# One level of Strassen in the second product of a fused attention and feed-forward kernel

## Chip, cores, metric

The kernel runs on one core of one Trainium2 chip. The metric is the device time of one execution in microseconds. The kernel before takes 303.68 us (median of 3 runs, 303.0 to 303.9). The span in a profile is 1.7 to 2.2 us shorter than the time of the same run.

## The reference

```python
# attention in chunks of 64 tokens: q, k, v are (8, 8, 576, 64), float32
scores = (1 / sqrt(64)) * q_c @ k_c.T;  attn = softmax(scores);  out = attn @ v_c
x = out.transpose(0, 2, 1, 3).reshape(4608, 512)
h = x @ w_in                       # 512 -> 2048
g = np.maximum(0.01 * h, h)
return g @ w_out                   # 2048 -> 512, float32
```

## The kernel before

The 4608 tokens go through in nine blocks of 512. TensorE runs the first product of block j (16 groups of 4 matmuls, `mm1`), then its second product (4 token groups of 16 matmuls, `mm2`). Between these groups, at fixed steps n, stand the four attention stages of block j+1 for each of four head pairs: `attn_t` (copies of q and k into matmul form, on VectorE), `attn_s` (scores), `attn_x` (sums and attn @ v) and `attn_n` (normalise into `xT`, on VectorE). GpSimd casts k, half of v and, up to block 3, q of later blocks to fp16; from block 4 on VectorE casts q. From block 3 on, the DMA transposes q and k; before that TensorE does.

```python
KD = [...]                                 # two block-diagonal buffers of k
def attn_t(j, kk):
    ...                                    # j < 3: TensorE transposes into PSUM (tp), VectorE copies qt
    for hh in range(2):                    # two copies of kd, 64 x 512 each
        nc.vector.tensor_copy(out=dst, in_=src)      # block 0: partly on ScalarE

def mm1_end(j, hp, fc):                    # ScalarE: leaky ReLU into g, fp16
    nc.scalar.activation(out=gT[j][:, fc, :], in_=hp, func=AFT.Prelu, ..., alpha=0.01)

def mm2(j, ti, part):                      # 4 matmuls of 512 columns
    for fc in range(part * 4, part * 4 + 4):
        nc.tensor.matmul(out=o, lhsT=gT[j][:, fc, ti * 128:(ti + 1) * 128],
                         rhs=w_out[:, fc, :], start=(fc == 0), stop=(fc == NFC - 1))
    if part == 3:
        nc.vector.tensor_copy(out=osb, in_=o)        # PSUM -> SBUF, then stored by DMA

for j in range(NJ):
    qk_at = {0: {26: 2}, 1: {0: 3, 29: 4}, 2: {15: 5}}.get(j, {9: j + 3})   # step: block whose q, k are loaded
    ...
    for n in range(...):                   # program order of all engines
        mm1(j, n) or mm2(j, ...)
        ...                                # loads, attention stages of block j + 1,
        ...                                # casts for block j + 2
```

PSUM has four banks for the products (tag `mm`) and four for the attention. w_in, w_out and g are fp16 in SBUF.

The softmax here doesn't subtract the row's maximum and nothing guards it: scores larger than these inputs give would overflow.

Of the kernel before, what the change touches and what calls it, by code (L numbers as in the profile page):

```python
# [8 lines left out]
FP16 = mybir.dt.float16  # L9
FP32 = mybir.dt.float32  # L10
ALU = mybir.AluOpType
AFT = mybir.ActivationFunctionType
# [3 lines left out]
def kernel(  # L16
# [9 lines left out]
    nc = tc.nc  # L26

    B, H, S, D = q.shape
    d_model, d_ff = moe_w_in.shape
# [3 lines left out]
    NKK = H // 2  # L33
    NFC = d_ff // 128
    TB = 512
    NJ = n_tok // TB
    NC = TB // CH
    R = 4
    NI = CH // R
    NPT = 3  # L40
    SCL = float(D) ** -0.5

    sb = ctx.enter_context(tc.tile_pool(name="sb", bufs=1))
    ps = ctx.enter_context(tc.tile_pool(name="ps", bufs=1, space=bass.MemoryType.PSUM))
# [14 lines left out]
    NVD = 2  # L59
    KD = [sb.tile([128, NC, 2, CH], FP16, name=f"kd{m}") for m in range(NKD)]  # L60
    VD = [sb.tile([128, NKK, NC, 2, CH], FP16, name=f"vd{m}") for m in range(NVD)]
# [11 lines left out]
    w_out = sb.tile([128, NFC, d_model], FP16, name="w_out")  # L73
# [3 lines left out]
    def segments(j):  # L77

        t, end = j * TB, (j + 1) * TB
        while t < end:  # L80
            b, s = divmod(t, S)
            n = min(end - t, S - s)
            yield t - j * TB, n, b, s
            t += n
# [9 lines left out]
    def sbuf(shape, dtype, name, bufs):  # L94
        return sb.tile(shape, dtype, name=name, tag=name, bufs=bufs)

    def psum(shape, dtype, name, tag):
        return ps.tile(shape, dtype, name=name, tag=tag, bufs=4)


    def alloc(j):
        raw[j] = (
            sbuf([128, H, R * D], FP32, "qf", 2),
            sbuf([128, H, R * D], FP32, "kf", 2),
            sbuf([128, NKK, NC, D], FP32, "vf", 2),
        )
        half[j] = tuple(sbuf([128, NKK, R, 2, D], FP16, n, 2) for n in ("qh", "kh"))

# [14 lines left out]
    def load_v(j, h, eng):  # L123

        kk, hh = divmod(h, 2)
        rows = slice(hh * CH, (hh + 1) * CH)
        dmas = []
        for off, n, b, s in segments(j):
            cs = slice(off // CH, (off + n) // CH)
            if eng is nc.gpsimd:  # L130
                dst = VD[j % NVD][rows, kk, cs, hh, :]
            else:
                dst = raw[j][2][rows, kk, cs, :]
            dmas.append(
                eng.dma_start(  # L135
                    out=dst, in_=v[b, h, s:s + n, :].rearrange("(c p) d -> p c d", p=CH)
                )
            )
        return dmas
# [19 lines left out]
    def cast_v(j, kk):  # L159
        for hh in range(2):  # L160
            rows = slice(hh * CH, (hh + 1) * CH)
            dst, src = VD[j % NVD][rows, kk, :, hh, :], raw[j][2][rows, kk, :, :]
            nc.gpsimd.tensor_copy(out=dst, in_=src)  # L163

    def transpose(j):
# [36 lines left out]
    def attn_s(j, kk):  # L202
# [11 lines left out]
        e = sbuf([128, R, 128], FP16, "e", 4)  # L214
        nc.scalar.activation(out=e, in_=sp, func=AFT.Exp, bias=0.0, scale=SCL)  # L215
        live[j, kk] = e

    def attn_x(j, kk):

        e = live[j, kk]  # L220
        zp = psum([128, TB], FP32, "zp", "at")
        nc.tensor.matmul(out=zp, lhsT=onesd, rhs=e, start=True, stop=True)  # L222
        xp = psum([128, R, 128], FP32, "xp", "at")
        for c in range(NC):
            nc.tensor.matmul(  # L225
                out=xp[:, :, c * NI:(c + 1) * NI],
                lhsT=VD[j % NVD][:, kk, c, :, :],
                rhs=e[:, :, c * NI:(c + 1) * NI],
                start=True,
                stop=True,  # L230
            )
        lz = sbuf([128, TB], FP32, "lz", 2)
        nc.scalar.activation(out=lz, in_=zp, func=AFT.Ln, bias=0.0, scale=1.0)  # L233
        rz = sbuf([128, TB], FP32, "rz", 2)
        nc.scalar.activation(out=rz, in_=lz, func=AFT.Exp, bias=0.0, scale=-1.0)  # L235
        live[j, kk] = (xp, rz)

    def attn_n(j, kk):
# [10 lines left out]
    def mm1_part(j, hp, fc, kk):  # L249
        nc.tensor.matmul(  # L250
            out=hp,
            lhsT=w_in[:, kk, fc * 128:(fc + 1) * 128],
            rhs=xT[j][:, kk, :],
            start=(kk == 0),
            stop=(kk == NKK - 1),
        )
# [8 lines left out]
    def mm1(j, fc):  # L265
        hp = psum([128, TB], FP32, "hp", "mm")
        for kk in range(NKK):
            mm1_part(j, hp, fc, kk)
        mm1_end(j, hp, fc)

    def mm2(j, ti, part):
        if part == 0:
            op[j, ti] = psum([128, d_model], FP32, "op", "mm")
        o = op[j, ti]
        for fc in range(part * 4, part * 4 + 4):
            nc.tensor.matmul(  # L276
                out=o,
                lhsT=gT[j][:, fc, ti * 128:(ti + 1) * 128],
                rhs=w_out[:, fc, :],
                start=(fc == 0),  # L280
                stop=(fc == NFC - 1),
            )
        if part == 3:
            osb = sbuf([128, d_model], FP32, "osb", 4)
            nc.vector.tensor_copy(out=osb, in_=o)  # L285
            nc.sync.dma_start(
                out=out[j * TB:(j + 1) * TB, :].rearrange("(p r) m -> r p m", r=R)[ti],
                in_=osb,
            )

    def keep_warm(n):
        for _ in range(n):
# [9 lines left out]

    def load_pairs(j, eng, pairs):
        return [d for h in pairs for hh in range(2) for d in load_v(j, 2 * h + hh, eng)]

    SW, HW = (0, 1), (2, 3)

    with tc.manual_schedule():

# [8 lines left out]
        for step in range(NKK + 2):  # L318
# [10 lines left out]
            p = step - 2  # L329
            if 0 <= p < NKK:  # L330
                attn_x(0, p)
            p = step - 1
# [4 lines left out]
            p = step - 2  # L337
# [27 lines left out]
        for kk in HW:  # L365
            cast_v(1, kk)

        def regular(first, gap, lags=(0, 3, 5, 7)):
            return [[first + gap * kk + lag for kk in range(NKK)] for lag in lags]
# [2 lines left out]

        for j in range(NJ):

            qk_at = {0: {26: 2}, 1: {0: 3, 29: 4}, 2: {15: 5}}.get(j, {9: j + 3})
            hw_at = {0: {26: 2}, 1: {1: 3}, 2: {0: 4, 16: 5}}.get(j, {10: j + 3})
            sw_at = {0: 26, 1: 10}.get(j, 10)
            cast_at = {0: 34, 1: 20, 2: 6}.get(j, 0)
            tr_at = cast_at + 8
            steps = {  # L380
                0: [[10, 14, 18, 22], [13, 17, 21, 25], [25, 26, 27, 28], [27, 28, 29, 30]],
                1: regular(9, 4, (0, 3, 7, 9)),
                2: regular(4, 6),
            }.get(j, regular(0, 7))
            at: dict[int, list] = {}
            if j + 1 < NJ:
                for s in (3, 2, 1, 0):
                    for kk in range(NKK):
                        at.setdefault(steps[s][kk], []).append((STEPS[s], kk))
            for n in range(2 * NFC + (16 if j == 0 else 0)):  # L390
                if n >= 2 * NFC:
                    pass
                elif n >= NFC:
                    ti, part = divmod(n - NFC, 4)
                    mm2(j, *((part, ti) if j == 0 else (ti, part)))
                elif j or n >= len(hps):
                    mm1(j, n)
                if qk_at.get(n, NJ) < NJ:
                    alloc(qk_at[n])
                    if j > 0:  # L400
                        load_qk(qk_at[n], 0, H)
                    else:
                        first = load_qk(qk_at[n], 0, H // 2)[0]
                        load_qk(qk_at[n], H // 2, H)
                        after(first, last, "the first two blocks' operands come first")
                for n0, jl in hw_at.items():
                    if j == 0 and n == n0:
                        load_pairs(jl, nc.sync, HW)
                    elif 0 < j and jl < NJ and n - n0 in range(0, 8, 2):
                        load_v(jl, 4 + (n - n0) // 2, nc.sync)  # L410
                for stage, kk in at.get(n, ()):
                    stage(j + 1, kk)
                if j + 2 < NJ:
                    if n in range(cast_at, cast_at + 8, 2):
                        kk = (n - cast_at) // 2
                        cast_qk(0, j + 2, kk, nc.vector if j > 1 else nc.gpsimd)
                        cast_qk(1, j + 2, kk, nc.gpsimd)
                        if kk in HW:
                            cast_v(j + 2, kk)
                    if n in range(sw_at, sw_at + 8, 2):  # L420
                        load_v(j + 2, (n - sw_at) // 2, nc.gpsimd)
                    if NPT <= j + 2 and n == tr_at:
                        transpose(j + 2)
# [30 lines left out]
```

## Time and profile before

| | before |
|---|---|
| time, median | 303.68 us |
| TensorE busy | 95% of the span |
| first products of blocks 1, 2, 3 start at | 54.62, 87.12, 118.23 us |
| period of blocks 3 to 7 | 30.35 us |
| second-product half of a steady block | 15.18 us |

The lines that this rests on stand in the prediction.

### The profile page before, as it was taken

To read this page: it belongs to the slowest core of one execution; us is meant where nothing else is said; L and a number is where in the kernel's file an instruction comes from. 1 tells how busy PE (TensorE), PEld (TensorE's weight loads), DVE (VectorE), ACT (ScalarE), POOL (GpSimd) and SP (SyncE) were. 2 spreads that over 40 slices of the span, in tenths; PEclk is the share of its full clock that TensorE was granted. 3 is DMA by queue.
4 is the path that set the end of the run, shared out by engine and by line. 5 is a ranking of instruction groups with operands and counts; after the bars stand their busy time and mean duration, and the time that the engine had idled before them with its cause. 6 is when DMAs were issued, how large, how long until landed. Compare 5 with 4: busy or idle time off the path is not lost.

```text
span 302.0 us, 4847 instructions
## 1 busy us (share of the span) xinstructions
PE 287.2 (95%) x1880; PEld 140.2 (46%) x1880; DVE 111.3 (37%) x186; ACT 148.8 (49%) x256; POOL 102.2 (34%) x165
## 2 busy tenths in 40 slices
PE   5769989999999999999999999999999999999994
PEld 2534435455544444454445444544454445444441
DVE  6560442425521644424462444254424422420011
ACT  2665506464437733872387228732873287327400
POOL 5764656584620480480490191055000000000000
PEclk9999999999999999999999999999999999999999
DMA  8999998999989999999989969957701100110011
GB/s 194 231 170 241 246 209 185 209 225 201 195 166 216 205 166 212 222 166 228 240 152 230 203 150 165 298 104 109 155 4 48 66 27 0 40 69 32 0 72 69
DMA packets 92599, 46.20 MB, mean 153 GB/s; under 512 B 65440, under 2 KB 87968, under 8 KB 92576
## 3 DMA queue, kind: packets, MB, share of 16 engines
q1 hardware_dynamic: 68896, 39.33, 58.1%
q0 software_dynamic: 23680, 6.56, 21.2%
q8 instruction: 15, 0.25, 0.3%
q14 instruction: 8, 0.07, 0.1%
HBM read 36.70 MB, written 9.44 MB: 153 GB/s over the span
## 4 chain that ended last, share of the span: by engine, by line
PE 67%; DMA 23%; POOL 4%; SPq 3%; issue 1%; DVE 1%; POOLq 0%; DVEq 0%
PE op L276 32%; PE hp L250 30%; DMA kf<-in_k_dram 10%; DMA w_out<-in_moe_w_out_dram 7%; DMA vd_76<-in_v_dram 2%; DMA kT<-kh 2%; SPq L114 2%; PE sp L207 2%; PE xp L225 2%; PE zp L222 2%; POOL kh L154 1%; DMA vf<-in_v_dram 1%; POOL vd_75 L163 1%; POOL vd_76 L163 1%; POOL w_in L143 1%
## 5 line engine op out<-in xcount | busy, mean ns | idle before, releaser
L276 PE MATMUL op<-w_out,gT 128*128 128x512 f16 x576 | 132.2, 379 | 1.5 <-DMA w_out<-in_moe_w_out_dram 1.5
L250 PE MATMUL hp<-xT,w_in 128*128 128x512 f16 x576 | 131.3, 379 | 2.2 <-DMA w_in<-in_moe_w_in_dram 2.0
L261 ACT ACTIVATE gT<-hp 128x512 f16<-128x512 f32 x144 | 84.8, 596 | 60.1 <-PE hp L250 59.9
L250 PEld LDWEIGHTS <-w_in 128*128 128x128 f16 x576 | 54.2, 98 | 64.1 <-DMA w_in<-in_moe_w_in_dram 3.5
L276 PEld LDWEIGHTS <-gT 128*128 128x128 f16 x576 | 53.7, 98 | 60.6 <-issue 1.8
L285 DVE COPY osb<-op 128x512 f32<-128x512 f32 x36 | 24.9, 690 | 81.1 <-PE op L276 81.0
L154 POOL CAST kh<-kf 128x512 f16<-128x512 f32 x36 | 22.0, 627 | 87.4 <-DMA kf<-in_k_dram 87.1
L243 DVE TENSOR_TENSOR xT<-xp,rz 128x512 f16<-128x512 f32 x36 | 24.8, 690 | 58.2 <-ACT rz L235 53.9
L215 ACT ACTIVATE e<-sp 128x512 f16<-128x512 f32 x36 | 21.3, 592 | 36.0 <-PE sp L207 36.0
L233 ACT ACTIVATE lz<-zp 128x512 f32<-128x512 f32 x36 | 21.4, 595 | 32.3 <-PE zp L222 32.1
L235 ACT ACTIVATE rz<-lz 128x512 f32<-128x512 f32 x36 | 22.7, 630 | 1.7 <-DVE xT L243 0.6
L135 POOL DMA_DIRECT2D vd_76<-in_v_dram x32 | 21.7, 695 | 2.1 <-DMA w_out<-in_moe_w_out_dram 2.1
L135 POOL DMA_DIRECT2D vd_75<-in_v_dram x32 | 20.8, 680 | 0.3 <-issue 0.3
L187 DVE COPY qt<-tp 128x512 f16<-128x512 f16 x12 | 5.1, 425 | 34.2 <-PE tp L183 34.2
L199 DVE COPY kd_73<-kT 64x512 f16<-64x512 f16 x24 | 14.6, 609 | 5.8 <-DMA kT<-kh 5.5
L199 DVE COPY kd_74<-kT 64x512 f16<-64x512 f16 x24 | 16.3, 677 | 0.4
L163 POOL CAST vd_75<-vf 64x512 f16<-64x512 f32 x20 | 14.0, 701 | 3.6 <-PE xp L225 2.1
L222 PE MATMUL zp<-e,onesd 128*128 128x512 f16 x36 | 13.6, 379 | 0.7 <-ACT e L215 0.7
L154 POOL CAST qh<-qf 128x512 f16<-128x512 f32 x15 | 9.2, 612 | 7.9 <-DMA qf<-in_q_dram 7.7
L163 POOL CAST vd_76<-vf 64x512 f16<-64x512 f32 x16 | 10.0, 626 | 4.5 <-DMA vf<-in_v_dram 4.1
L154 DVE CAST qh<-qf 128x512 f16<-128x512 f32 x21 | 9.5, 501 | 3.5 <-DMA qf<-in_q_dram 3.4
L225 PEld LDWEIGHTS <-vd_75 128*128 128x128 f16 x160 | 7.3, 98 | 5.7 <-POOL vd_75 L163 1.0
(44 smaller groups left out, 104.7 us busy)
## 6 DMA issues: line engine op xcount, KB each, us to landing
out_dram<-osb SPq DMA_DIRECT2D x36, 256.0 KB, 2.7
w_in<-in_moe_w_in_dram POOLq DMA_DIRECT2D x4, 512.0 KB, 8.9
w_out<-in_moe_w_out_dram POOLq DMA_DIRECT2D x4, 512.0 KB, 13.5
qf<-in_q_dram SPq DMA_DIRECT2D x4, 384.0 KB, 6.6
kf<-in_k_dram SPq DMA_DIRECT2D x4, 384.0 KB, 10.3
qf<-in_q_dram SPq DMA_DIRECT2D x5, 256.0 KB, 6.1
kf<-in_k_dram SPq DMA_DIRECT2D x5, 256.0 KB, 6.6
qf<-in_q_dram SPq DMA_DIRECT2D x2, 640.0 KB, 7.7
```

Of the source, the lines that this page charges most:

```text
L135: eng.dma_start(out=dst, in_=v[b, h, s:s + n, :].rearrange("(c p) d -> p c d", p=CH))
L154: eng.tensor_copy(out=half[j][a][:, kk, :, :, :], in_=raw[j][a][:, 2 * kk:2 * kk + 2, :].rearrange("p h (r d) -> p r h d", r=R),)
L163: nc.gpsimd.tensor_copy(out=dst, in_=src)
L199: nc.vector.tensor_copy(out=dst, in_=src)
L215: nc.scalar.activation(out=e, in_=sp, func=AFT.Exp, bias=0.0, scale=SCL)
L233: nc.scalar.activation(out=lz, in_=zp, func=AFT.Ln, bias=0.0, scale=1.0)
L235: nc.scalar.activation(out=rz, in_=lz, func=AFT.Exp, bias=0.0, scale=-1.0)
L243: nc.vector.tensor_tensor(out=xT[j][:, kk, :], in0=xp.rearrange("p r t -> p (r t)"), in1=rz, op=ALU.mult)
L250: nc.tensor.matmul(out=hp, lhsT=w_in[:, kk, fc * 128:(fc + 1) * 128], rhs=xT[j][:, kk, :], start=(kk == 0), stop=(kk == NKK - 1),)
L261: nc.scalar.activation(out=gT[j][:, fc, :], in_=hp, func=AFT.Prelu, bias=0.0, scale=1.0, alpha=0.01)
L276: nc.tensor.matmul(out=o, lhsT=gT[j][:, fc, ti * 128:(ti + 1) * 128], rhs=w_out[:, fc, :], start=(fc == 0), stop=(fc == NFC - 1),)
L285: nc.vector.tensor_copy(out=osb, in_=o)
```

## The change

The intent: the second product of blocks 1 to 8 is split in halves of tokens, of f and of output columns, and is made from 7 products of quarters in place of 8 (Strassen's scheme: the products M1 to M7 are of sums of quarters, and sums of the products give the result). A quarter of g is the even or the odd groups of 128 rows of f, for one half of the tokens; the layout of g stays. VectorE makes the sums of g in every block (two of the five in place) and those of w_out once (three into new buffers in block 0, two in place at the start of block 1). The products are evacuated by ScalarE (M3, M4) and by sums on VectorE that read PSUM. To have room and data in time, block 3's q and k are loaded behind block 2's, ahead of block 2's v; casts, transposes and attention steps of blocks 1 and 2 are moved; v's fp32 buffer is halved and one fp32 buffer of the softmax goes.

```diff
+    def g_sums(j, g):                       # on VectorE, 5 x 512 fp16 elements, four times a block
+        a11, a12, a21, a22 = (x[:, i, :] for x in g_quarters(j))
+        tt(nc.vector, gs["a11_12"][:, i, :], a11, a12, ALU.add)
+        tt(nc.vector, gs["a21_22"][:, i, :], a21, a22, ALU.add)
+        tt(nc.vector, gs["a11_22"][:, i, :], a11, a22, ALU.add)
+        tt(nc.vector, a21, a21, a11, ALU.subtract)
+        tt(nc.vector, a12, a12, a22, ALU.subtract)
+    def product(o, a, b, u):                # 8 matmuls of 256 columns
+        for i in range(NH):
+            nc.tensor.matmul(out=o, lhsT=a[:, i, u * 128:(u + 1) * 128], rhs=b[:, i, :], ...)
+    def mm2s(j, u, step):                   # u: 128 tokens of each half; step: M3 M4 M5 M2 M1 M6 M7
+        if step == 0:
+            product(bank("M3"), a11, b12_22, u)
+            nc.scalar.activation(out=keep("m3"), in_=part["M3"], func=AFT.Copy, ...)
+        ...
+        elif step == 2:
+            product(bank("M5"), gs["a11_12"], b22, u)
+            tt(V, part["top"][:, hi], part["M5"], part["m3"], add)
+            tt(V, keep("m45"), part["m4"], part["M5"], sub)
+        ...
-            qk_at = {0: {26: 2}, 1: {0: 3, 29: 4}, 2: {15: 5}}.get(j, {9: j + 3})
-            hw_at = {0: {26: 2}, 1: {1: 3}, 2: {0: 4, 16: 5}}.get(j, {10: j + 3})
-            sw_at = {0: 26, 1: 10}.get(j, 10)
-            cast_at = {0: 34, 1: 20, 2: 6}.get(j, 0)
+            qk_at = {0: {25: 2, 26: 3}, 1: {20: 4}, 2: {15: 5}}.get(j, {9: j + 3})
+            hw_at = {0: {27: 2}, 1: {20: 3}, 2: {0: 4, 16: 5}}.get(j, {10: j + 3})
+            sw_at = {0: 26, 1: 23}.get(j, 10)
+            cast_at = {0: 34, 1: 11, 2: 6}.get(j, 0)
-                1: regular(9, 4, (0, 3, 7, 9)),
-                2: regular(4, 6),
+                1: [[7, 11, 17, 20], [10, 14, 20, 23], [14, 18, 23, 26], [16, 20, 25, 28]],
+                2: regular(9, 4),
+                if j and n in (4, 8, 12, 16):
+                    g_sums(j, n // 4 - 1)
+                if j == 0 and n in (20, 23, 26, 32):
+                    w_sums((n - 20) // 3 if n < 32 else 3, nc.vector)
+                if j == 1 and n < 4:
+                    w_in_place(n, nc.vector)
```

More of the change, by code (lines that the diff above doesn't have):

```diff
@@ L41 @@
     SCL = float(D) ** -0.5
+    SW, HW = (0, 1), (2, 3)
     sb = ctx.enter_context(tc.tile_pool(name="sb", bufs=1))
@@ L104, in alloc @@
             sbuf([128, H, R * D], FP32, "kf", 2),
-            sbuf([128, NKK, NC, D], FP32, "vf", 2),
+            sbuf([128, len(HW), NC, D], FP32, "vf", 2),
         )
@@ L132, in load_v @@
             else:
-                dst = raw[j][2][rows, kk, cs, :]
+                dst = raw[j][2][rows, HW.index(kk), cs, :]
             dmas.append(
@@ L161, in cast_v @@
             rows = slice(hh * CH, (hh + 1) * CH)
-            dst, src = VD[j % NVD][rows, kk, :, hh, :], raw[j][2][rows, kk, :, :]
+            dst, src = VD[j % NVD][rows, kk, :, hh, :], raw[j][2][rows, HW.index(kk), :, :]
             nc.gpsimd.tensor_copy(out=dst, in_=src)
@@ L231, in attn_x @@
             )
-        lz = sbuf([128, TB], FP32, "lz", 2)
-        nc.scalar.activation(out=lz, in_=zp, func=AFT.Ln, bias=0.0, scale=1.0)
         rz = sbuf([128, TB], FP32, "rz", 2)
-        nc.scalar.activation(out=rz, in_=lz, func=AFT.Exp, bias=0.0, scale=-1.0)
+        nc.scalar.activation(out=rz, in_=zp, func=AFT.Ln, bias=0.0, scale=1.0)
+        nc.scalar.activation(out=rz, in_=rz, func=AFT.Exp, bias=0.0, scale=-1.0)
         live[j, kk] = (xp, rz)
@@ L285, in mm2, with tt @@
             nc.vector.tensor_copy(out=osb, in_=o)
-            nc.sync.dma_start(
-                out=out[j * TB:(j + 1) * TB, :].rearrange("(p r) m -> r p m", r=R)[ti],
-                in_=osb,
-            )
+            store(j, ti, osb)
+    NH = NFC // 2
+    MH = d_model // 2
+    wv = w_out.rearrange("p (i e) (h m) -> p e h i m", e=2, h=2)
+    ws = {n: sb.tile([128, NH, MH], FP16, name=f"ws_{n}") for n in ("b11_22", "b11_12", "b21_11")}
+    gs: dict[str, bass.AP] = {}
+    def tt(eng, out, in0, in1, op):
+        eng.tensor_tensor(out=out, in0=in0, in1=in1, op=op)
@@ new lines, in w_sums, with w_in_place @@
+    def w_sums(g, eng):
+        i = slice(2 * g, 2 * g + 2)
+        b11, b12, b21, b22 = (wv[:, e, h, i, :] for e in range(2) for h in range(2))
+        tt(eng, ws["b11_22"][:, i, :], b11, b22, ALU.add)
+        tt(eng, ws["b11_12"][:, i, :], b11, b12, ALU.add)
+        tt(eng, ws["b21_11"][:, i, :], b21, b11, ALU.subtract)
+    def w_in_place(g, eng):
+        i = slice(2 * g, 2 * g + 2)
+        tt(eng, wv[:, 0, 1, i, :], wv[:, 0, 1, i, :], wv[:, 1, 1, i, :], ALU.subtract)
+        tt(eng, wv[:, 1, 0, i, :], wv[:, 1, 0, i, :], wv[:, 1, 1, i, :], ALU.add)
@@ new lines, in g_quarters @@
+    def g_quarters(j):
+        gv = gT[j].rearrange("p (i e) (h t) -> p h e i t", e=2, h=2)
+        return [gv[:, h, e, :, :] for h in range(2) for e in range(2)]
+    def g_sums(j, g):
+        if g == 0:
+            for n in ("a11_12", "a21_22", "a11_22"):
+                gs[n] = sbuf([128, NH, TB // 2], FP16, n, 1)
+        i = slice(2 * g, 2 * g + 2)
+        a11, a12, a21, a22 = (x[:, i, :] for x in g_quarters(j))
[4 more added lines that the diff above has]
+        tt(nc.vector, a12, a12, a22, ALU.subtract)
@@ new lines, in product, with store, bank, keep @@
+    def product(o, a, b, u):
+        for i in range(NH):
+            nc.tensor.matmul(
+                out=o,
+                lhsT=a[:, i, u * 128:(u + 1) * 128],
+                rhs=b[:, i, :],
+                start=(i == 0),
+                stop=(i == NH - 1),
+            )
+    def store(j, ti, osb):
+        nc.sync.dma_start(
+            out=out[j * TB:(j + 1) * TB, :].rearrange("(p r) m -> r p m", r=R)[ti], in_=osb
+        )
+    part: dict[str, bass.AP] = {}
+    def mm2s(j, u, step):
+        a11, a21_11, a12_22, a22 = (g_quarters(j)[n] for n in (0, 2, 1, 3))
+        b11, b12_22, b21_22, b22 = wv[:, 0, 0], wv[:, 0, 1], wv[:, 1, 0], wv[:, 1, 1]
+        lo, hi = slice(0, MH), slice(MH, d_model)
+        def bank(n):
+            part[n] = psum([128, d_model], FP32, "mp", "mm")[:, lo]
+            return part[n]
+        def keep(n):
+            part[n] = sbuf([128, MH], FP32, n, 2)
+            return part[n]
+        V, add, sub = nc.vector, ALU.add, ALU.subtract
+        if step == 0:
+            for n in ("top", "bot"):
+                part[n] = sbuf([128, d_model], FP32, "osb", 4)
+            product(bank("M3"), a11, b12_22, u)
+            nc.scalar.activation(out=keep("m3"), in_=part["M3"], func=AFT.Copy, bias=0.0, scale=1.0)
+        elif step == 1:
+            product(bank("M4"), a22, ws["b21_11"], u)
+            nc.scalar.activation(out=keep("m4"), in_=part["M4"], func=AFT.Copy, bias=0.0, scale=1.0)
+        elif step == 2:
+            product(bank("M5"), gs["a11_12"], b22, u)
+            tt(V, part["top"][:, hi], part["M5"], part["m3"], add)
+            tt(V, keep("m45"), part["m4"], part["M5"], sub)
+        elif step == 3:
+            product(bank("M2"), gs["a21_22"], b11, u)
+            tt(V, part["bot"][:, lo], part["M2"], part["m4"], add)
+            tt(V, keep("m32"), part["m3"], part["M2"], sub)
+        elif step == 4:
+            product(bank("M1"), gs["a11_22"], ws["b11_22"], u)
+            tt(V, keep("m132"), part["M1"], part["m32"], add)
+            tt(V, keep("m145"), part["M1"], part["m45"], add)
+        elif step == 5:
+            product(bank("M6"), a21_11, ws["b11_12"], u)
+            tt(V, part["bot"][:, hi], part["M6"], part["m132"], add)
+            store(j, 2 + u, part["bot"])
+        else:
+            product(bank("M7"), a12_22, b21_22, u)
+            tt(V, part["top"][:, lo], part["M7"], part["m145"], add)
+            store(j, u, part["top"])
@@ L304, in load_pairs @@
         return [d for h in pairs for hh in range(2) for d in load_v(j, 2 * h + hh, eng)]
-    SW, HW = (0, 1), (2, 3)
     with tc.manual_schedule():
@@ L393 @@
                 elif n >= NFC:
-                    ti, part = divmod(n - NFC, 4)
-                    mm2(j, *((part, ti) if j == 0 else (ti, part)))
+                    if j == 0:
+                        mm2(j, *reversed(divmod(n - NFC, 4)))
+                    elif n - NFC < 14:
+                        mm2s(j, *divmod(n - NFC, 7))
                 elif j or n >= len(hps):
                     mm1(j, n)
+                if hw_at.get(n, NJ) < NJ:
+                    load_pairs(hw_at[n], nc.sync, HW)
                 if qk_at.get(n, NJ) < NJ:
                     alloc(qk_at[n])
-                    if j > 0:
+                    if j > 0 or n > 25:
                         load_qk(qk_at[n], 0, H)
@@ L405 @@
                         after(first, last, "the first two blocks' operands come first")
-                for n0, jl in hw_at.items():
-                    if j == 0 and n == n0:
-                        load_pairs(jl, nc.sync, HW)
-                    elif 0 < j and jl < NJ and n - n0 in range(0, 8, 2):
-                        load_v(jl, 4 + (n - n0) // 2, nc.sync)
                 for stage, kk in at.get(n, ()):
                     stage(j + 1, kk)
+                if j and n in (4, 8, 12, 16):
[4 more added lines that the diff above has]
+                    w_in_place(n, nc.vector)
                 if j + 2 < NJ:
@@ L417 @@
                         cast_qk(1, j + 2, kk, nc.gpsimd)
-                        if kk in HW:
+                        if kk in HW and j > 1:
                             cast_v(j + 2, kk)
+                    if j == 1 and n in (cast_at + 7, 30):
+                        for kk in HW:
+                            cast_v(2 + (n == 30), kk)
                     if n in range(sw_at, sw_at + 8, 2):
```

## The prediction

> **What bounds the kernel now.** I read the page's first two parts, then the chain, then the groups, and last the timelines of single engines in one steady block.
>
> ```profile
> span 302.0 us, 4847 instructions
> PE 287.2 (95%) x1880; PEld 140.2 (46%) x1880; DVE 111.3 (37%) x186; ACT 148.8 (49%) x256; POOL 102.2 (34%) x165
> PE   5769989999999999999999999999999999999994
> DVE  6560442425521644424462444254424422420011
> PEclk9999999999999999999999999999999999999999
> DMA  8999998999989999999989969957701100110011
> ```
>
> TensorE is full from the seventh slice on, at full clock; VectorE has room; the DMA engines are loaded until slice 28. A loaded DMA is a bound only if somebody waits for it, so next the chain and the groups:
>
> ```profile
> PE op L276 32%; PE hp L250 30%; DMA kf<-in_k_dram 10%; DMA w_out<-in_moe_w_out_dram 7%; DMA vd_76<-in_v_dram 2%; DMA kT<-kh 2%; SPq L114 2%; PE sp L207 2%; PE xp L225 2%; PE zp L222 2%; POOL kh L154 1%; DMA vf<-in_v_dram 1%; POOL vd_75 L163 1%; POOL vd_76 L163 1%; POOL w_in L143 1%
> L276 PE MATMUL op<-w_out,gT 128*128 128x512 f16 x576 | 132.2, 379 | 1.5 <-DMA w_out<-in_moe_w_out_dram 1.5
> L250 PE MATMUL hp<-xT,w_in 128*128 128x512 f16 x576 | 131.3, 379 | 2.2 <-DMA w_in<-in_moe_w_in_dram 2.0
> L285 DVE COPY osb<-op 128x512 f32<-128x512 f32 x36 | 24.9, 690 | 81.1 <-PE op L276 81.0
> L243 DVE TENSOR_TENSOR xT<-xp,rz 128x512 f16<-128x512 f32 x36 | 24.8, 690 | 58.2 <-ACT rz L235 53.9
> ```
>
> The DMA share of the chain lies before 94 us. After that the chain is nothing but matmuls, and the second product (L276) is 576 of them in nine blocks, 64 a block. This is the second-product half of a steady block in the TensorE timeline (start, length, instructions):
>
> ```profile
> 161.17 2.75 PE L250 MATMUL hp<-xT,w_in 128*128 128x512 f16 x12
> 163.76 1.89 PE L276 MATMUL op<-w_out,gT 128*128 128x512 f16 x8
> 165.49 0.40 PE L207 MATMUL sp<-qT,kd_73 128*128 128x64 f16 x8
> 165.72 1.89 PE L276 MATMUL op<-w_out,gT 128*128 128x512 f16 x8
> ...
> 174.62 4.48 PE L276 MATMUL op<-w_out,gT 128*128 128x512 f16 x20
> 178.94 3.62 PE L250 MATMUL hp<-xT,w_in 128*128 128x512 f16 x16
> ```
>
> The lengths have modelled ends; the starts are what counts. Eight matmuls of 512 columns take 165.49 - 163.76 = 1.73 us, 216 ns each; eight of 64 columns take 0.23 us, 29 ns each. The half lasts 15.18 us = 64 x 0.216 + 1.36 for the attention steps of the next block, so it has no hole at all. A block repeats every 30.35 us (first products start at 148.6 and 178.94).
>
> **What the Trainium skill says.** First, "TensorE: Matmul & The Clock Gate", section Back-to-back issue gap: a warm matmul takes N / 2.4 GHz + 2.5 ns, so 216 ns at 512 columns and 109.2 ns at 256. It adds that in a stream of pairs of load and matmul the load counts too, about 81 ns for N = 128. The trace agrees with the formula at 64 and 512 columns, and not with the 81 ns: the transposes, 128 columns each behind a new weight load, follow each other after 56 to 57 ns (33.71 to 33.94 for four, below). So at 256 columns a weight load per matmul should stay hidden.
>
> ```profile
> 33.71 0.39 PE L183 MATMUL tp<-ident,qh 128*128 128x128 f16 x4
> 33.94 0.39 PE L183 MATMUL tp<-ident,kh 128*128 128x128 f16 x4
> ```
>
> Second, "VectorE: DVE Perf Modes", the perf-mode tier table and the errata section: tensor_tensor on 16-bit SBUF data makes two elements a cycle, with a PSUM operand one, and an fp32 add lasts (N + 151) / 0.96 ns. The 690 ns of L243 at 512 fp32 elements from PSUM are exactly that. No tensor_tensor with two 16-bit SBUF operands is in this trace, so its double rate is taken from the page.
>
> Third, "SBUF — State Buffer", section Who interferes with whom: a VectorE instruction with two SBUF inputs contends with a GpSimd instruction that reads SBUF. Nothing here shows it for tensor_tensor, but VectorE's casts show a like effect: four take 1.43 us in one block and 2.98 us in another where GpSimd casts at the same time.
>
> **The change, part by part.**
>
> TensorE: blocks 1 to 8 get 7 products x 2 halves of 128 tokens x 8 steps of f = 112 matmuls of 256 columns instead of 64 of 512. 112 x 0.1092 = 12.23 us against 64 x 0.216 = 13.82: 1.59 us less a block, 12.7 us in eight blocks. This is on the path.
>
> VectorE per block: 4 evacuations (L285) go. 20 sums of g come, 512 fp16 elements each; by the page (256 + 151) / 0.96 = 424 ns long, an estimate. Neighbouring instructions overlap: L243 and L285 of 690 ns start 600 ns apart when back to back, so I take 90 ns off: 0.335 us of the engine each, 6.7 us. 16 combinations of a PSUM half bank with SBUF, 256 fp32 elements each, come to the same 424 ns: 5.4 us. What stays is 4 xT (0.60), 8 copies of kd (0.61) and 4 casts (0.34 to 0.75): 8.7 to 10.3 us. The sum is 21 to 22.5 us in a block of 28.8 us, three quarters: no bound by itself, but no longer idle. ScalarE gets 4 copies a block, estimated 0.4 us each at half the elements of its 0.6 us operations: 1.6 us beside a present 16 of 30 us. Harmless.
>
> Waits inside a block. The last activation of g starts 0.2 us after the second product begins (163.96 against 163.76) and takes 0.6. M3 and M4, which need no sum, cover the first 1.75 us; M5 needs only the first of the five last sums, ready about 1.3 us in; its last group is read at 2.4 us. That fits. PSUM has four banks in rotation, filled every 0.87 us and emptied by two instructions of 0.335, so VectorE may lag by more than two products. The tightest place is the end: xT of the last head pair is normalised only at n = 28, one product before the block ends, where it had three groups. From the end of M6: 0.2 us to the combination, 0.33 for it, 0.69 for xT, 1.25 to 1.3 in all; the next first product reads it after M7 and three matmuls, 0.87 + 0.65 = 1.52 us. It holds by 0.2 us, and any lag of VectorE eats that. I allow 0.25 us a block: 2 us.
>
> Sums of w_out: 12 instructions in block 0 and 8 in place in block 1, 20 x 0.335 = 6.7 us of VectorE while it is 40% busy. I count nothing on the path.
>
> Loading early: block 3's q and k follow block 2's in the queue, ahead of block 2's v. At present TensorE is held up there:
>
> ```profile
> 94.77 0.41 PE L207 MATMUL sp<-qT,kd_73 128*128 128x64 f16 x8 [0.58 <-DVE kd_73 L199]
> ```
>
> That 0.6 us goes. In return v of block 2 comes behind 2 MB of q and k, some 10 us at the 200 GB/s of the page, and is needed two products earlier; I allow 0.7 us. Steady blocks have room: block 6's transposes were in by 166 us and first read at 179.
>
> The tail: the last evacuation is 0.42 us instead of 0.69: 0.3 less.
>
> Sum: 303.7 - 12.7 - 0.6 - 0.3 + 2.0 + 0.7 = 292.8. Loads and waits are retuned by hand in the diff, which says that my allowances were seen to; I take 292.0.
>
> **Rivals.**
>
> 1. VectorE becomes the bound. If the fp16 sums ran at one element a cycle, 20 x 0.6 = 12 us instead of 6.7, it would be busy 26 to 28 of 28.8 us, and every local queue (the 28th step, kd before each score) would hold TensorE up. For it: contention with GpSimd's casts, and nothing in the trace proves the double rate. Against it: all operands are 16-bit runs of 256. It would make 297 to 303 us.
>
> 2. A new wait at the seam. The in-place differences of g write into runs that lie between the runs M4 reads. If the waits do not tell these apart, M4 waits for all five last sums: 0.8 + 1.75 us against 1.5, at least 1 us a block, 300 us or more. Against it: the four quarters share no element and the order of products is visibly chosen for this seam.
>
> 3. The loads bound the early part. DMA is at nine tenths until 200 us; TensorE that runs 1.6 us a block faster catches up with it. For it: the present 0.58 us wait and 12 us waits of GpSimd for kf in every block. Against it: those loads are started by steps of TensorE's own program and have 13 us of slack in steady state. Blocks 1 and 2 alone might lose 1 to 3 us: 293 to 295.
>
> 4. Weight loads show. If a pair at 256 columns took 118 ns instead of 109, 8 us of the 12.7 would go: 300. The 56 ns of the transposes speak against it.
>
> **Range and chances.** With no new wait the sum is 290; with mild forms of rivals 1 and 3, 295 to 296. I say 289.5 to 296.5. Two per cent faster is 297.6; it is missed only if rival 1, 2 or 4 is real, together some 13%, and slower than before by 2% would need two of them.
>
> **What would show it.** Right: groups of seven lines of products with 256 columns, eight starts 0.87 us apart, 112 a block; a period of blocks 4 to 7 near 28.8 us; VectorE at 65 to 80% of the span, fp16 sums of 0.42 us; the second-product half near 13.6 us. Wrong: sums of 0.69 us, or much longer ones beside GpSimd (rival 1); an idle before M4 released by VectorE (rival 2); idle before zp, xp or sp of block 2 or 3 (rival 3); products more than 0.87 us apart with no wait named (rival 4); idle before hp released by xT at each block's start (my 28th step).

## More of the kernel before

One view more, the kernel before in stretches, one a block (block 1, 2 and 3). Its columns are the stretch, its length, then for each engine busy time and instructions, the granted clock, the DMA share and GB/s.

```profile
54.62:87.12 32.50, 32.30 (x229) 16.56 (x228) 13.04 (x22) 16.40 (x28) 19.10 (x32) 1.00 1.10 195
87.12:118.23 31.11, 30.53 (x198) 14.69 (x196) 12.07 (x20) 16.35 (x28) 10.03 (x16) 1.00 1.10 197
118.23:148.59 30.36, 30.36 (x198) 14.77 (x197) 12.15 (x20) 16.08 (x28) 11.28 (x18) 1.00 1.23 211
```

The first number after the comma is TensorE, the third VectorE: TensorE fills the stretch, VectorE works 12 to 13 us of it.

## The result and the profile after

294.86 us (median of 4 runs, 294.4 to 295.55) against 303.79 in the same rounds: ratio 0.9708, 95% interval 0.9674 to 0.9742, so 2.9% faster. A ratio here is the mean time of one kernel's fast runs over that of the other's of the same rounds, so it is not quite the ratio of the medians. The time lies within the range; the expected 292.0 was 2.9 us too low.

The page of the changed kernel, first two parts:

```profile
span 292.7 us, 5954 instructions
PE 276.3 (94%) x2264; PEld 177.8 (61%) x2264; DVE 210.7 (72%) x462; ACT 159.9 (55%) x288; POOL 108.0 (37%) x165
DVE  5560455998974998798799779787778748863554
```

VectorE went from 37% to 72% of the span, and in slices 8 to 12, where block 1 runs, it stands at 9, 9, 8, 9 and 7. The TensorE timeline of the second-product half of a steady block:

```profile
162.59 1.04 PE L333 MATMUL mp<-w_out,gT 128*128 128x256 f16 x8
163.46 1.04 PE L333 MATMUL mp<-ws_b_11_87,gT 128*128 128x256 f16 x8
164.33 0.40 PE L209 MATMUL sp<-qT,kd_73 128*128 128x64 f16 x8
...
175.30 1.04 PE L333 MATMUL mp<-w_out,gT 128*128 128x256 f16 x8
176.18 3.62 PE L251 MATMUL hp<-xT,w_in 128*128 128x512 f16 x16
```

Products start 0.87 us apart and the half lasts 176.18 - 162.59 = 13.59 us, as predicted (13.6). Nothing waits in it. The same stretches as before (blocks 1, 2 and 3) tell where it went less well:

```profile
53.75:87.89 34.14, 31.24 (x277) 21.12 (x276) 31.37 (x65) 17.78 (x32) 21.57 (x33) 1.00 1.11 190
87.89:118.64 30.75, 29.30 (x247) 19.22 (x245) 24.47 (x53) 17.91 (x32) 11.78 (x18) 1.00 1.13 208
118.64:147.41 28.77, 28.77 (x247) 19.48 (x245) 23.77 (x53) 17.40 (x32) 11.71 (x16) 1.00 1.12 213
```

Block 3 takes 28.77 us, all TensorE, and so do blocks 4 to 7. Block 1 is longer than before, 34.14 against 32.50 us, and VectorE is busy for 31.37 us of it. In blocks 1 and 2 of the timeline TensorE waits five times for more than 0.3 us, always before a score, always for a copy of kd on VectorE (the brackets give idle time and releaser; three are in block 1, two in block 2):

```profile
65.18 0.41 PE L209 MATMUL sp<-qt,kd_73 128*128 128x64 f16 x8 [0.96 <-DVE kd_73 L201]
77.43 0.41 PE L209 MATMUL sp<-qt,kd_73 128*128 128x64 f16 x8 [1.13 <-DVE kd_73 L201]
81.96 0.41 PE L209 MATMUL sp<-qt,kd_74 128*128 128x64 f16 x8 [0.61 <-DVE kd_74 L201]
104.45 0.41 PE L209 MATMUL sp<-qT,kd_74 128*128 128x64 f16 x8 [1.02 <-DVE kd_74 L201]
109.20 0.41 PE L209 MATMUL sp<-qT,kd_73 128*128 128x64 f16 x8 [0.40 <-DVE kd_73 L201]
```

Counted from start to start (the ends of matmuls are modelled), these and one of 0.2 us are 5.2 us of lost time in blocks 1 and 2. What VectorE did before the second of them, and GpSimd beside it:

```profile
72.28 0.46 DVE L298 TENSOR_TENSOR a_12_795<-gT 128x512 f16<-128x512 f16 x1 [0.28 <-ACT gT L262]
72.66 0.83 DVE L298 TENSOR_TENSOR a_22_796<-gT 128x512 f16<-128x512 f16 x1
73.41 0.82 DVE L298 TENSOR_TENSOR a_22_797<-gT 128x512 f16<-128x512 f16 x1
74.16 1.57 DVE L298 TENSOR_TENSOR gT<-gT 128x512 f16<-128x512 f16 x2
75.66 0.41 DVE L189 COPY qt<-tp 128x512 f16<-128x512 f16 x1
75.99 1.38 DVE L201 COPY kd_73<-tp 64x512 f16<-64x512 f16 x2
```

```profile
72.41 0.80 POOL L156 CAST qh<-qf 128x512 f16<-128x512 f32 x1
73.16 0.80 POOL L156 CAST kh<-kf 128x512 f16<-128x512 f32 x1
```

The first sum takes 0.46 us, the others about 0.8: GpSimd's casts of block 3 run beside them, and these too take 0.80 us instead of 0.61. In block 8, where GpSimd is done, the sums take 0.42 us on average. In the whole trace, the 146 sums with two inputs in SBUF and no cast of GpSimd beside them took 0.41 to 0.43 us; of the 34 beside a cast, 26 took more than 0.6. VectorE's copies of kd from SBUF stretch too: 0.60 us alone, 0.93 beside a cast (medians of 40 and 8). The queue then holds the copies of kd back until 77.37. The theory after reading: **the gain is TensorE's, fewer columns streamed; the loss in blocks 1 and 2 is a queue at VectorE, stretched where its two-input sums meet GpSimd's casts.** Rivals: the early loads bring part of the gain; the waits come from data that arrives late; Strassen pays in all blocks alike and the waits have nothing to do with its work.

### The profile page after: what moved, and what is told of

It is laid out like the page before. It is cut to its first block, busy times and chain, and to the rows that moved or that the text cites. A ratio compares the mean times of both kernels' runs of the same rounds, so it can differ in the third digit from the quotient of the medians.

```text
span 292.7 us, 5954 instructions
## 1 busy us (share of the span) xinstructions
PE 276.3 (94%) x2264; PEld 177.8 (61%) x2264; DVE 210.7 (72%) x462; ACT 159.9 (55%) x288; POOL 108.0 (37%) x165
## 4 chain that ended last, share of the span: by engine, by line
PE 67%; DVE 4%; ACT 0%; issue 0%
PE hp L251 31%; PE mp L333 30%; PE sp L209 2%; PE xp L227 2%; PE zp L224 2%; DVE kd_74 L201 1%; DVE gT L298 1%; DVE kd_73 L201 1%; DVE qh L156 1%; DVE a_12_1291 L298 0%; DVE a_22_1292 L298 0%; DVE a_22_1293 L298 0%; ACT gT L262 0%; DVE osb L298 0%
## 5 line engine op out<-in xcount | busy, mean ns | idle before, releaser
L333 PEld LDWEIGHTS <-gT 128*128 128x128 f16 x512 | 49.8, 98 | 7.4
L156 POOL CAST kh<-kf 128x512 f16<-128x512 f32 x36 | 24.7, 701 | 77.8 <-DMA kf<-in_k_dram 77.5
L235 ACT ACTIVATE rz<-zp 128x512 f32<-128x512 f32 x36 | 21.4, 595 | 28.0 <-PE zp L224 26.8
L333 PE MATMUL mp<-w_out,gT 128*128 128x256 f16 x256 | 32.0, 273 | 0.0
L298 DVE TENSOR_TENSOR gT<-gT 128x512 f16<-128x512 f16 x64 | 26.2, 449 | 0.0
L236 ACT ACTIVATE rz<-rz 128x512 f32<-128x512 f32 x36 | 22.7, 631 | 1.1
L137 POOL DMA_DIRECT2D vd_76<-in_v_dram x32 | 22.0, 702 | 2.2 <-DMA w_out<-in_moe_w_out_dram 2.2
L137 POOL DMA_DIRECT2D vd_75<-in_v_dram x32 | 21.4, 691 | 0.3 <-issue 0.3
L277 PE MATMUL op<-w_out,gT 128*128 128x512 f16 x64 | 15.4, 379 | 1.5 <-DMA w_out<-in_moe_w_out_dram 1.5
L333 PE MATMUL mp<-ws_b_12_86,gT 128*128 128x256 f16 x128 | 16.6, 273 | 0.0
L333 PE MATMUL mp<-ws_b_11_87,gT 128*128 128x256 f16 x128 | 16.6, 273 | 0.0
L165 POOL CAST vd_75<-vf 64x512 f16<-64x512 f32 x20 | 13.7, 684 | 2.0 <-DMA vf<-in_v_dram 1.3
L165 POOL CAST vd_76<-vf 64x512 f16<-64x512 f32 x16 | 11.3, 709 | 8.1 <-DMA vf<-in_v_dram 7.7
L224 PE MATMUL zp<-e,onesd 128*128 128x512 f16 x36 | 13.6, 379 | 0.7 <-ACT e L217 0.7
```

Source lines behind the costliest of these rows:

```text
L137: eng.dma_start(out=dst, in_=v[b, h, s:s + n, :].rearrange("(c p) d -> p c d", p=CH))
L156: eng.tensor_copy(out=half[j][a][:, kk, :, :, :], in_=raw[j][a][:, 2 * kk:2 * kk + 2, :].rearrange("p h (r d) -> p r h d", r=R),)
L165: nc.gpsimd.tensor_copy(out=dst, in_=src)
L235: nc.scalar.activation(out=rz, in_=zp, func=AFT.Ln, bias=0.0, scale=1.0)
L236: nc.scalar.activation(out=rz, in_=rz, func=AFT.Exp, bias=0.0, scale=-1.0)
L298: eng.tensor_tensor(out=out, in0=in0, in1=in1, op=op)
```

## The experiments

Eleven runs followed, on three chips: ten edited kernels and the change once more. A ratio is to the kernel before. "Wait" below is lost time from start to start on TensorE in the profiled run. Times of one kernel scatter by 1 to 4 us from run to run, fast runs alone; the start of block 1 in the traces lies between 52.7 and 55.2 us, whatever the kernel, because the weights arrive sooner or later. So stretches between block starts say more than totals.

### The earlier loads alone

```diff
-                    elif n - NFC < 14:
-                        mm2s(j, *divmod(n - NFC, 7))
+                    else:
+                        mm2(j, *divmod(n - NFC, 4))
-  (all sums of g and w_out)
```

> The earlier loads and the new steps alone, second product as before. My theory: the loads are worth only the 0.6 to 0.75 us that TensorE waited for block 3's first copy of k, so 303.1 us, ratio to before 0.998, and a steady period of 30.35 us. Rival (a good part of the gain is the earlier loading): 300 us or less.

Measured: 303.13 us, ratio 1.0002 (0.9962 to 1.0042), period 30.35 us; the wait before block 3's first score fell only from 0.74 to 0.60 us, so that gain hardly came. The first rival falls: by itself the earlier loading is worth nothing that can be measured.

### Strassen with the loads of before

```diff
-            qk_at = {0: {25: 2, 26: 3}, 1: {20: 4}, 2: {15: 5}}.get(j, {9: j + 3})
+            qk_at = {0: {26: 2}, 1: {0: 3, 29: 4}, 2: {15: 5}}.get(j, {9: j + 3})
-            cast_at = {0: 34, 1: 11, 2: 6}.get(j, 0)
+            cast_at = {0: 34, 1: 20, 2: 6}.get(j, 0)
-                2: regular(9, 4),
+                2: regular(4, 6),
   (and the places of v's loads and casts)
```

> The Strassen products with the loads, casts and block 3's steps of the kernel before. My theory: the holes of blocks 1 and 2 are a queue at VectorE, lengthened where its sums of g meet GpSimd's casts; with the casts of block 3 back at a later time, the hole of 1.3 us before the third score of block 1 goes or falls under 0.4, the one of 1.1 us before the first stays (the sums of w_out are still there), and block 3's first score waits 1.5 to 2.5 us for its transposes instead. Sum 294 to 296 us. Rival (the Strassen products are only fast because the data comes early): 298 us or more.

Measured: 297.14 and 298.26 us in the two fast runs (two others were slow and are left out), ratio 0.9816, called unclear. The sum was a miss. Block 1 took 31.31 us instead of 34.14: the wait before its third score went, as expected, and so did the one before its first, which was not expected. There the casts met fewer sums: the eight in-place sums of w_out took 2.76 us in place of 3.58. But block 2 took 36.08 us: 1.54 us of wait for block 3's transposes, as expected, and then 3.48 us, which I had not foreseen. Behind that stop came 0.92 us of wait for a sum, and the matmuls of 512 columns followed each other after 0.43 us in place of 0.216 for some 2.5 us, another 1.3 us. VectorE's cast of block 4's q stood at the head of its queue and waited 4.03 us for data asked for nine steps later than in the change; the sums and the next copy of kd stood behind it. So the second rival is half right: the earlier loads, with the casts and steps that moved with them, are worth nothing alone, and some 3 us (by these two fast runs) with the Strassen products, as these reach the same steps sooner and put more work behind each late item of VectorE's queue.

### Strassen only from block 3 on

```diff
+                    elif j < 3:
+                        mm2(j, *divmod(n - NFC, 4))
-                if j and n in (4, 8, 12, 16):
+                if j >= 3 and n in (4, 8, 12, 16):
-                if j == 1 and n < 4:
+                if j == 3 and n < 4:
                     w_in_place(n, nc.vector)
```

> Strassen from block 3 on, plain products in blocks 0 to 2, the in-place sums of w_out moved to the start of block 3. My theory: in blocks 1 and 2 the change lost 1.3 us against before instead of gaining 3.2, as 5.2 us of waits for VectorE ate it; without it there these two blocks take about 62.9 us instead of 64.9, all else equal: 292.9 us, faster than the change by 2 us. Rival (Strassen pays in every block, the waits have another cause, such as the casts, the transposes or data that comes late): the waits stay and 3.2 us are lost: 298 us.

Measured: 294.75 us, ratio 0.9712 (0.9659 to 0.9766): the same as the change with its 0.9708. The waits for kd of block 1 are gone; blocks 1 and 2 take 63.99 us against the change's 64.89, not the 62.9 expected, since block 2's first score waited 1.1 us behind a cast of block 4's q, which stood 9.5 us at the head of VectorE's queue for its data. And block 3, which now holds the in-place sums, waits 0.95 and 0.41 us before its scores and takes 30.15 us instead of 28.77. The loss moves with VectorE's work. Two blocks of Strassen, which should save 3.2 us, are worth nothing in blocks 1 and 2 as they stand.

### Half of the copies of kd on ScalarE

```diff
-            if j == 0 and kk < 3 and hh == 0:
+            if (j == 0 and kk < 3 or j in (2, 3)) and hh == 0:
                 nc.scalar.activation(out=dst, in_=src, func=AFT.Copy, bias=0.0, scale=1.0)
```

> The change, with half of the copies of kd for blocks 2 and 3 (8 of 16, 0.6 to 0.7 us each) on ScalarE. My theory (VectorE's queue makes the waits before the scores in blocks 1 and 2): the waits fall from 5.2 us to 1.5 to 2.5, and the time to about 291.8 us. Rival (what comes late is the data: q and k, their casts on GpSimd, the transposes): the waits and the 294.9 us stay.

Measured: 293.55 us (293.1 to 293.97), ratio 0.9684 (0.9647 to 0.9720), by the time alone not told apart from the change; waits of 1.64, 0.83 and 0.36 us, 2.8 in all. In block 1 they fell only from 3.2 to 2.5 us: there the timelines show VectorE's half of the copy starting only when ScalarE's had ended, and ScalarE's only when VectorE's copy of qt had. All three read the same PSUM bank; whether that is the reason, no run shows. In block 2, where the source is in SBUF, the waits fell from 2.0 to 0.4 us.

### Casts held until the sums are done

```diff
-            cast_at = {0: 34, 1: 11, 2: 6}.get(j, 0)
+            cast_at = {0: 34, 1: 17, 2: 6}.get(j, 0)
+            t = nc.gpsimd.tensor_copy(out=dst, in_=src)      # first cast of v behind block 1's sums
+            after(t, last_sum[0], "GpSimd reads nothing while VectorE sums")
```

> The change with GpSimd's casts for block 3 held until block 1's last sum of g is done; nothing is taken off VectorE. My theory (the sums take double time while GpSimd casts beside them): the five last sums take 0.42 us each instead of 0.82, so the wait of 1.3 us before block 1's third score goes or falls under 0.3, and the other waits stay: 293.7 us. Rival (the queue is just too long, contention or not): the sums stay at 0.8 us and the wait stays.

VectorE's timeline of the same place in this run:

```profile
72.53 1.09 DVE L302 TENSOR_TENSOR a<-gT 128x512 f16<-128x512 f16 x3 [0.28 <-ACT gT L266]
73.55 0.42 DVE L302 TENSOR_TENSOR gT<-gT 128x512 f16<-128x512 f16 x1
73.88 0.42 DVE L333 TENSOR_TENSOR gT<-gT 128x512 f16<-128x512 f16 x1
74.22 0.41 DVE L193 COPY qt<-tp 128x512 f16<-128x512 f16 x1
74.55 1.38 DVE L205 COPY kd<-tp 64x512 f16<-64x512 f16 x2
```

Five sums in 1.7 us instead of 3.4, and no wait before the third score. With nothing taken off VectorE, the sums alone got shorter: what stretched them was GpSimd. Blocks 1 and 2 of this run as stretches:

```profile
55.15:86.45 31.30, 30.88 (x277) 21.31 (x276) 27.39 (x65) 17.55 (x32) 18.34 (x28) 1.00 1.01 191
86.45:122.18 35.73, 31.45 (x246) 20.33 (x244) 23.34 (x53) 17.95 (x32) 14.11 (x21) 0.90 1.17 196
```

Block 1 took 31.30 us, with VectorE busy for 27.4 us of it and one wait of 0.38 us before a score. So "the other waits stay" was a miss, to the good: the wait before the first score was gone, which the edit doesn't explain, as it leaves the casts of block 2 where they were. They met fewer sums here, and one of them took 2.49 us while the sums beside it stayed at 0.42. The wait before the first score is missing in the change's own repeat too. The time was a miss as well: 296.85 us, ratio 0.9758 (0.9708 to 0.9807), called unclear and no better than the change, as block 3's transposes came later and its first score waited 4.4 us. After that stop 512-column matmuls again took 0.43 us each, for some 5 us and at a cost of 2.5 us; the granted clock of the stretch is 0.90. That cost I had not counted.

### VectorE relieved

```diff
+            if j == 2 and kk >= 2:                      # block 2's last two head pairs
+                nc.scalar.activation(out=qt, in_=tp[:, 0, :, :], func=AFT.Copy, bias=0.0, scale=1.0)
-            if j == 0 and kk < 3 and hh == 0:
+            if (j == 0 and kk < 3 or j == 3) and hh == 0 or j == 2 and kk >= 2:
-                if j and n in (4, 8, 12, 16):
+                g_at = (8, 9, 12, 16) if j == 1 else (4, 8, 12, 16)
```

> The change with VectorE relieved where it was late: the third and fourth copies of block 2's q and k out of PSUM wholly on ScalarE (the run with half of them there showed that a bank is copied by one engine after the other), half of block 3's copies of k on ScalarE, and block 1's first sums of g behind its first copy of k. My theory (a queue at VectorE): the waits before scores in blocks 1 and 2 fall from 5.2 to under 1.5 us, blocks 1 and 2 take 60 to 61.5 us instead of 64.9, and the time is 290.5 to 291.5 us. Rival (data that comes late): 294 us or more.

The change itself ran beside it:

> The change unaltered, on the same chip as the three below, so that they can be compared with it. 294.9 us, with the start of block 1 anywhere from 52.7 to 54.8 us (the arrival of the weights differs from run to run) and 3 to 5.5 us of waits for VectorE in blocks 1 and 2.

Measured: 292.27 us, ratio 0.9634 (0.9600 to 0.9669), against 295.17 us and 0.9712 (0.9668 to 0.9757) for the change; by the means of their fast runs, 292.05 and 294.41, it is 2.4 us faster (the two intervals just touch). Blocks 1 and 2 take 61.92 us, block 1 of them 31.00 without a wait before a score. The direction was right and each number a little short: waits of 2.2 us were left in place of 1.5, all in block 2. In the change's own repeat they took 63.31 us, with 3.6 us of waits for kd. What was left stands in block 2. VectorE and TensorE in the relieved run:

```profile
94.23 0.43 DVE L156 CAST qh<-qf 128x512 f16<-128x512 f32 x1 [3.38 <-DMA qf<-in_q_dram]
...
96.70 0.59 DVE L204 COPY kd<-kT 64x512 f16<-64x512 f16 x1
```

```profile
97.39 0.39 PE L212 MATMUL sp<-qT,kd 128*128 128x64 f16 x8 [1.55 <-ACT gT L265]
```

The bracket names ScalarE, which had long been done with the g in question; the copy of kd ended at 97.29, and it had stood behind a cast that waited 3.38 us for q. To test that, the casts were put behind the copy:

```diff
-                    if n in range(cast_at, cast_at + 8, 2):
-                        kk = (n - cast_at) // 2
+                    if n in (range(10, 14) if j == 2 else range(cast_at, cast_at + 8, 2)):
+                        kk = n - 10 if j == 2 else (n - cast_at) // 2
```

> The relieved version, with VectorE's casts of block 4's q put behind its first copy of k for block 3 (in the run before, the 1.7 us wait of block 2 came from such a cast, which waited 3.4 us for q at the head of VectorE's queue). If that is right, the wait before block 2's first score falls under 0.4 us and the time to 290.5 to 291.3 us. If the copy of k waits for its transposes or for ScalarE, the wait stays and the time is 292.3 us.

Measured: that wait is gone (a later score waits 0.85 us), block 2 takes 29.69 us. But the time is 291.94 us, ratio 0.9640 (0.9597 to 0.9683), the same as without it: in the profiled run GpSimd's casts came in the middle of block 3's sums (the third group's five took 3.3 us instead of 1.7), and block 3 waited 1.75 us before a score. The cause is confirmed, the gain is not. A second variant:

```diff
-            if (j == 0 and kk < 3 or j == 3) and hh == 0 or j == 2 and kk >= 2:
+            if j == 0 and kk < 3 and hh == 0 or j == 2 and kk >= 2:
```

> The same, but block 3's copies of k wholly on VectorE again. ScalarE took 1.1 us for each from SBUF, VectorE takes 0.6. If ScalarE's copies help, this is slower by 0.5 to 1 us than the run beside it, with a wait of 0.5 to 1 us before the second and third scores of block 2; if they only delay g, it is the same or faster.

Measured: 292.93 us, ratio 0.9675 (0.9645 to 0.9706), with waits of 0.89 and 1.12 us before scores of block 2. The direction is as expected, but the intervals of the two overlap, so the worth of ScalarE's copies for block 3 is left open.

### Sums made twice

```diff
+        for _ in range(2 if j > 3 else 1):              # three of the five sums of g
             tt(nc.vector, gs["a11_12"][:, i, :], a11, a12, ALU.add)
```

> The change with three of the five sums of g made twice from block 4 on, so 12 more instructions of 0.335 us in a block, 4 us of VectorE. My theory: VectorE is busy 20 to 24 of 28.77 us there and hidden; with 4 us more it is near the bound, and the period grows by 0 to 1.5 us through waits for kd or for the sums. If the period were already set by VectorE (rival 1 of the prediction), it would grow by 4 us.

Measured (one run, state unknown, so only its periods are read): blocks 4 to 7 take 30.93, 29.47, 29.15 and 29.09 us instead of 28.77. With 4 us more of VectorE the period grows by 0.3 to 0.7 us, and by 2.2 in block 4, more than expected (1.11, 0.45 and 0.56 us of waits for kd and for a sum). It never grows by the whole 4 us: VectorE does not set it, and the room is nearly used up.

### The old product in two column halves

```diff
-            for fc in range(part * 4, part * 4 + 4):     # blocks 1 to 8
-                nc.tensor.matmul(out=o, ..., rhs=w_out[:, fc, :])
+            for fc in range(part % 2 * 8, part % 2 * 8 + 8):
+                nc.tensor.matmul(out=o[:, ms], ..., rhs=w_out[:, fc, ms])   # ms: one half of 256 columns
```

> The kernel before, with its second product of blocks 1 to 8 in two column halves: 128 matmuls of 256 columns a block for the same result, no Strassen. My theory (time is columns streamed, 109.2 ns a matmul of 256): 13.98 us a block against 13.82, period 30.5 us, 1.3 us longer in all, 305 us. Rival (a weight load per 256 columns shows, 118 ns): 15.1 us, period 31.6 us, 313 us.

Its TensorE timeline:

```profile
163.58 1.91 PE L281 MATMUL op<-w_out,gT 128*128 128x256 f16 x16
165.33 0.40 PE L207 MATMUL sp<-qT,kd 128*128 128x64 f16 x8
```

Sixteen matmuls of 256 columns in 1.75 us, 109.4 ns each, and a period of 30.52 us (block starts at 178.92 and 209.44) against 30.35. The time of one run, 304.44 us (state unknown), agrees. Twice as many weight loads cost 0.16 us a block: the narrow form is neutral, and all the gain comes from 112 such matmuls in place of 128.

## Why the prediction was right, and where it was not

The spans of the two kernels, by block starts, against the terms of the sum:

| stretch | before | after | difference | predicted |
|---|---|---|---|---|
| to the start of block 1 | 54.62 | 53.75 | -0.87 | 0 |
| blocks 1 and 2 | 63.61 | 64.89 | +1.28 | -2.6 |
| blocks 3 to 7 | 151.78 | 143.85 | -7.93 | -6.7 |
| block 8 and the end | 31.99 | 30.21 | -1.78 | -1.6 |
| sum | 302.0 | 292.7 | -9.3 | -10.9 |

(The predicted column spreads the prediction's sum: 1.59 us a block, 0.25 back for waits, the 0.6 and 0.7 of the loads in blocks 1 and 2, the 0.3 of the end.)

- **The main term held to the hundredth.** 1.59 us a block was predicted; blocks 3 to 7 gained 7.93 / 5 = 1.59. Narrow matmuls take what the formula gave, shown by themselves in the kernel of two halves. Rival 4 is out.
- **The rate of the fp16 sums**, which no trace had shown, was right: 0.42 us. So were ScalarE's copies (0.38 against 0.4) and VectorE's share (72% of the span, 65 to 80 said). Rivals 1 and 2 as whole-kernel bounds are out: no product waited at the seam in a steady block, and 4 us more of sums lengthen the period by 0.3 to 2.2 us.
- **The 28th step**, called the tightest place, cost nothing: in the block shown, xT is done at 176.53 us and its matmul starts 3 x 0.216 after 176.18, at 176.83. The slack of 0.2 us held (it is 0.3), and the 2 us allowed for it were not needed.
- **The step that failed** is "the sums of w_out: I count nothing on the path", with "no bound by itself" worked out for a steady block (21 to 22.5 us of 28.8) and carried to blocks 1 and 2. The sum held 0.5 us for waits there and 0.7 for the loads; it should have held 5.2 us (3.6 in the repeat). Block 1 has more on VectorE than a steady block: 11 sums of w_out, and copies out of PSUM, qt among them. From the view before: 13.0 us busy there, less 2.8, plus 47 sums (20, 16 and 11) at the prediction's 0.335, is 26 us of a block of 31. That is tight and still fits: the run with the casts held had 27.4 us and 0.4 us of waits before scores. In the change it was 31.4 us. So the term that was mis-sized is the 0.335 us of a sum: beside GpSimd's casts sums started 0.75 us apart. All waits before scores of block 1 go when work is taken off VectorE (Strassen from block 3 on, the relieved version); the largest, 1.3 us before the third score, goes also when only the casts are held. So that one takes both, the load and the stretching. The one before the first score comes and goes from run to run, with where block 2's casts fall.
- **Contention** was named under rival 1, though as a threat to the whole kernel. It acts, but only where data happens to arrive: GpSimd's casts are released by DMA, not by a step. Holding them back made the five sums short again, which shows it.
- **The sign of rival 3** (idle before sp of block 2 or 3) came, and the loss has the size that it gave. But what the scores waited for was a copy of kd, and VectorE waits for no DMA in blocks 1 and 2 of the change: it is the local queue of rival 1, not the loads.
- **Early loading** was put at 0.6 us by itself. It is worth nothing measurable by itself and, by two fast runs, some 3 us together with the products. A part of a change that supports another can't be priced alone.
- That the time came so near is partly luck. Blocks 1 and 2 lost 3.9 us against the sum; 1.2 came back in blocks 3 to 7, where the allowance for waits was not needed, and 0.87 before block 1. These 0.87 us are not the change's: block 1 of the change's repeat starts at 53.66, of the loads-only run at 53.65, of others anywhere up to 55.15.

Open remain how block 2's 2.0 us of waits divide between load and stretching, the worth of ScalarE's copies for block 3, and whether any order of casts keeps all blocks clear of them.

## What to carry to other kernels

When work moves from a full engine to an idle one, sum the idle engine's work for each stage apart, the first ones above all: an engine at 83% in block 3 was at 92% in block 1, where the preparation fell, and there the gain was eaten. Price its instructions beside the other engines' work, too: 27 us of VectorE's work fitted into block 1 with the casts held, 31 did not. An in-order engine pays twice for an item that waits for data, once for the wait and once for what stands behind it (a cast of q that waited 3.4 us cost a score 1.7), so put casts of later blocks behind the copies that TensorE waits for next. A relief that takes copies off the late engine (here the last two head pairs of block 2 and half of block 3's copies of kd to ScalarE, with block 1's first sums behind its first copy) was worth 2.4 us on top of the 8.9 us of the change.

## What the Trainium skill lacked or had wrong

- "SBUF — State Buffer", Who interferes with whom: the page is right that a VectorE instruction with two SBUF inputs contends with a GpSimd one that reads SBUF, and calls the shared ports an exclusive lock, but gives no rate where both come in a row. Here sums went from 0.42 to 0.83 us and casts from 0.61 to 0.80, and each started every 0.75 us (0.335 and 0.56 alone). Sums with one input in PSUM stayed at 0.41 to 0.42 us beside casts, as the page has it.
- "TensorE: Matmul & The Clock Gate", Back-to-back issue gap: the page's 81 ns for a pair of weight load and matmul at 128 columns is not what runs here (56 to 57 ns); its formula N / 2.4 + 2.5 holds at 64, 256 and 512 columns with a new weight for each: 29, 109.2 to 109.4 and 216 ns.
- "VectorE: DVE Perf Modes", the errata section, gives ScalarE 224 + elements cycles from SBUF and 172 + elements from PSUM. ScalarE's copies of kd, 64 x 512 fp16 with a strided source, took 0.59 us from PSUM, near the page's 0.57, but 1.08 to 1.11 us from SBUF, where it gives 0.61; no run shows whether the stride is the reason.
